# Block 1's 256-column steps in pairs, wider identity products, and an order that counts TensorE's instructions

## The chip, the core and the metric

The kernel runs on one core of a Trainium2 chip. Five engines work side by side on their own instruction streams: TensorE (PE in the rows; its weight loads are a second track, PEld), VectorE (DVE), ScalarE (ACT), GpSimd (POOL) and SyncE (SP), which here issues the transfers. They meet only in semaphores. The metric is the device time of one execution in microseconds (us), the median of several runs.

## What is computed

A chunked attention with eight memory tokens feeds two feed-forward layers, all in fp32 on 3072 tokens:

```python
scores = scale * np.matmul(q_c, k_full.transpose(0, 1, 3, 2))   # 4 x 8 heads, 24 chunks of 32 queries
a = np.exp(scores - np.max(scores, axis=-1, keepdims=True))
a = a / (np.sum(a, axis=-1, keepdims=True) + 1e-09)
out[:, :, c_start:c_end] = np.matmul(a, v_full)
...
x = attn_out as 3072 x 512
h = x @ w_in            # 512 x 2048
g = h * np.clip(h + 3.0, 0.0, 6.0) / 6.0
x = g @ w_out           # 2048 x 512
h = x @ w_in2
g = np.maximum(0.01 * h, h)
return g @ w_out2
```

## The kernel before

**Feed-forward.** Tokens are cut into six blocks of 512 columns. A weight or an activation is held in two parts, a rounded high part and the rest, so that one product of 128 rows by 512 columns takes three groups of matmuls (high by high, low by high, high by low). For blocks 0 and 1 layer 1 goes step by step: for each of 16 slices `f` of the hidden dimension, `hidden` (matmuls at L910) makes 128 rows of h in the PSUM tile `h`, ScalarE adds three and clips (L922, tile `r`), VectorE multiplies (L925), ScalarE rounds to `g` (L318) and VectorE takes the rest (L321); `output` (matmuls at L954) adds the slice's product into the four PSUM tiles `y`. One step has 12 + 12 matmuls. The first four steps of block 1 are done on halves of 256 columns, because the second half of that block's tokens comes late out of the attention. Everything after those blocks is a Strassen form (L1229, L1397), which this change touches in its order alone.

**Weights.** They arrive as fp64 bits. `decode` and `split_w` turn each slice of 128 x 512 into a high and a low part: one ScalarE pass (L370), four VectorE passes (L373 to L385), a ScalarE cast (L318) and a VectorE subtraction (L321). Blocks 0 and 1 need a new pair of slices for each step.

**Attention.** Units of tokens, each one a chain: loads, copies of the keys into windows (L318), scores (a burst of 48 small fp32 matmuls of 32x64 outputs, L513, or 24, L743), maximum, exponentials (L549), sums, six transposes (L571, or three, L797), a copy (L318), the values (48 small fp32 matmuls of 64x32, L582, or 24, L810), and the split into block 0's or 1's operands `xh`, `xl`. The units' bursts are put between the feed-forward matmuls. In the first 35 us, before there is feed-forward work, products of the identity matrix with itself (`warm`, L439), which nobody reads, stand between the attention's bursts on TensorE.

**What sets the order.** No engine's order is written out. Each piece is a `Task` with engines, durations and a key; `schedule` plays them through with prices for engines, semaphores and transfers, and emits each instruction when its turn comes. So a changed price moves instructions on every engine. TensorE takes the task with the lowest key; an attention task that is ahead of its key is held while a feed-forward product is ready. A transfer counts as done at `wire + LANDS`.

## Time and profile before

| | us |
|---|---|
| median of three runs | 1052.82 (1051.19 to 1052.99) |
| the profiled execution, its own time | 1053.29 |
| its span, first to last instruction | 1051.50 |
| TensorE busy | 1030.8 |
| VectorE busy | 879.1 |
| ScalarE busy | 691.1 |

The profiled execution has 1.8 us outside its span and lies 0.5 us over the median. A row of a timeline or a window below starts with its time from the span's start; busy times of TensorE overlap, since matmuls are pipelined. An fp32 product (the attention's bursts and the identity products) is recorded as two matmuls, each with its weight load; the feed-forward's rounded operands take one.

### The profile page before, as it was taken

The page shows a single profiled execution, that of the slowest core. Times are in us where ns is not written, and L with a number is a line of the kernel's source. Part 1 is how long each engine was busy: PE and PEld are TensorE (multiplying, and loading weights), DVE is VectorE, ACT ScalarE, POOL GpSimd, SP SyncE. Part 2 cuts the span into 40 slices and gives each one's busy share as a digit, 9 for nine tenths or more (in the row PEclk, how much of TensorE's full clock was granted, in tenths as well). Part 3 has the DMA queues.
Part 4 walks back from the last instruction along what each step waited for, and adds up shares of the span by engine and source line. Part 5 has one row for each costly group of instructions (what it writes and reads, how often), then busy time and mean ns, then how long its engine had stood idle before and what let it go on. Part 6 is the DMA issues. An engine that isn't in the chain of part 4 may idle for free.

```text
span 1051.5 us, 20297 instructions
## 1 busy us (share of the span) xinstructions
PE 1030.8 (98%) x7528; PEld 854.6 (81%) x7528; DVE 879.1 (84%) x1493; ACT 691.1 (66%) x1444; POOL 23.8 (2%) x31
## 2 busy tenths in 40 slices
PE   7799999999999999999999999999999999999998
PEld 6678888888888888888888888888888888888886
DVE  5898898778999978799999899899475998466775
ACT  2687777555888745477686576786466884666753
POOL 3001000000000000000000000000000000000000
PEclk9899999999999999999999999999999999999999
DMA  9899788886878989872737875356342454432451
GB/s 231 276 246 323 226 279 263 252 263 239 276 250 268 296 269 325 278 242 96 240 121 261 268 238 194 122 178 206 117 177 84 159 197 165 163 119 90 150 180 60
DMA packets 127380, 220.50 MB, mean 210 GB/s; under 512 B 12593, under 2 KB 76081, under 8 KB 127281
## 3 DMA queue, kind: packets, MB, share of 16 engines
q1 hardware_dynamic: 127280, 219.20, 63.8%
q8 instruction: 59, 0.97, 0.4%
q14 instruction: 41, 0.33, 0.1%
HBM read 156.24 MB, written 62.91 MB: 208 GB/s over the span
## 4 chain that ended last, share of the span: by engine, by line
PE 90%; DMA 5%; DVE 2%; ACT 1%; SPq 1%; issue 1%; POOL 0%; DVEq 0%; ACTq 0%
PE y L1229 16%; PE y L954 13%; PE y L1397 12%; PE h L1229 10%; PE h L1397 8%; PE hx L1229 8%; PE hx L1397 8%; PE h L910 8%; DMA w<-in_raw 4%; PE h L954 2%; PE at L582 2%; PE at L513 1%; PE at L571 1%; DMA w<-in_w1o 1%; DMA w<-in_w1i 1%
## 5 line engine op out<-in xcount | busy, mean ns | idle before, releaser
L321 DVE TENSOR_TENSOR w<-w 128x512 fp32r<-128x512 f32 (+2 forms) x393 | 324.2, 861 | 24.9 <-ACT w L318 24.4
L318 ACT CAST w<-w 128x512 fp32r<-128x512 f32 (+1 forms) x290 | 223.5, 804 | 15.6 <-DMA w<-floats 6.7
L954 PE MATMUL y<-g,w 128*128 128x512 f32 (+1 forms) x540 | 124.7, 375 | 0.7 <-ACT w L318 0.4
L1229 PE MATMUL y<-w 128*128 128x512 f32 x516 | 124.3, 390 | 0.0
L1229 PEld LDWEIGHTS y<-w 128*128 128x128 f32 x516 | 96.7, 188 | 20.2
L954 PEld LDWEIGHTS y<-g,w 128*128 128x128 f32 x540 | 95.0, 189 | 19.6 <-ACT w L318 0.9
L318 ACT CAST g<-w 128x512 fp32r<-128x512 f32 x80 | 49.7, 622 | 64.8 <-PE y L1397 21.4
L1397 PE MATMUL y<-w 128*128 128x512 f32 x384 | 90.3, 389 | 0.0
L1397 PEld LDWEIGHTS y<-w 128*128 128x128 f32 x384 | 72.1, 188 | 15.0
L1203 ACT ACTIVATE w<-w 128x512 f32<-128x512 f32 x72 | 45.3, 632 | 44.5 <-DVE w L1274 18.9
L910 PE MATMUL h<-xh,w 128*128 128x512 f32 (+1 forms) x288 | 68.5, 379 | 0.6 <-DVE w L321 0.4
L321 DVE TENSOR_TENSOR g<-w,g 128x512 fp32r<-128x512 f32 x80 | 54.3, 688 | 12.5 <-ACT g L318 12.4
L1397 PE MATMUL h<-w 128*128 128x512 f32 x264 | 62.1, 389 | 0.0
L910 PEld LDWEIGHTS h<-xh,w 128*128 128x128 f32 x288 | 51.3, 196 | 10.6 <-DVE w L321 0.8
L1397 PE MATMUL hx<-w 128*128 128x512 f32 x252 | 59.2, 389 | 0.0
L1229 PE MATMUL h<-xl,w 128*128 128x512 f32 x240 | 58.3, 390 | 0.0
L1397 PEld LDWEIGHTS h<-w 128*128 128x128 f32 x264 | 49.5, 188 | 10.3
L1397 PEld LDWEIGHTS hx<-w 128*128 128x128 f32 x252 | 47.3, 188 | 9.8
L1229 PEld LDWEIGHTS h<-xl,w 128*128 128x128 f32 x240 | 44.8, 188 | 9.3
L1229 PE MATMUL y<-xh,w 128*128 128x512 f32 x216 | 51.9, 389 | 0.0
L1274 DVE TENSOR_TENSOR w<-y,w 128x512 f32<-128x512 f32 x35 | 24.0, 687 | 29.7 <-PE y L1229 27.0
L1229 PEld LDWEIGHTS y<-xh,w 128*128 128x128 f32 x216 | 40.5, 188 | 8.4
(242 smaller groups left out, 1868.6 us busy)
## 6 DMA issues: line engine op xcount, KB each, us to landing
w<-kept2i SPq DMA_DIRECT2D x42, 512.0 KB
w<-kept2o SPq DMA_DIRECT2D x42, 512.0 KB
w<-kept1i SPq DMA_DIRECT2D x28, 512.0 KB
a<-in_raw SPq DMA_DIRECT2D x20, 448.0 KB
w<-in_w1i SPq DMA_DIRECT2D x16, 512.0 KB
w<-in_w1o SPq DMA_DIRECT2D x16, 512.0 KB
w<-in_w2i SPq DMA_DIRECT2D x16, 512.0 KB
w<-in_w2o SPq DMA_DIRECT2D x16, 512.0 KB
```

The source lines that it names most:

```text
L318: nc.scalar.copy(out, in_) if e == "ACT" else engine(e).tensor_copy(out=out, in_=in_)
L321: engine(e).tensor_tensor(out=out, in0=a, in1=b, op=ALU.subtract)
L513: nc.tensor.matmul(ps.t[h * CHUNK:(h + 1) * CHUNK, par, i * W:(i + 1) * W], qk[h // 2].t[r, gp, (h % 2) * G + c * CHUNK:(h % 2) * G + (c + ...
L571: nc.tensor.transpose(pt.t[:, i // NC, (i % NC) * 128:(i % NC + 1) * 128], e.t[:, i].rearrange("p r k -> p (r k)"), ident)
L582: nc.tensor.matmul(pv.t[(h % 2) * D:(h % 2 + 1) * D, par, (h // 2) * 2 * G + i * CHUNK:(h // 2) * 2 * G + (i + 1) * CHUNK], v[h // 2].t[r, ...
L910: nc.tensor.matmul(h.t[:, :n], w.t[:, 1 if p == 1 else 0, k * 128:(k + 1) * 128], x[:, k, c0:c0 + n], start=(p == 0 and k == 0), stop=(p = ...
L954: nc.tensor.matmul(bank(banks[d])[:, c0:c0 + n], w.t[:, 1 if p == 1 else 0, d * 128:(d + 1) * 128], g.t[:, 1 if p == 2 else 0, :n], start= ...
L1203: return add(lambda e: nc.scalar.activation(out=at(), in_=at(), func=AF.Prelu, alpha=0.01), {"ACT": act(N)}, key, after=[after], uses=uses)
L1229: nc.tensor.matmul(bank(to), wt(l, o)[:, kt * 128:(kt + 1) * 128].bitcast(F32R), operand(p, name, 1 if q == 2 else 0, kt).bitcast(F32R), s ...
L1274: done[2] = add(lambda e: nc.vector.tensor_tensor(out=half_of(x, 0), in0=bank(bb), in1=ut.t[:, 0], op=ALU.add), low, key, after=[k, done[1 ...
L1397: nc.tensor.matmul(bank(to[d]), wt(1 if q == 1 else 0, o)[:, d * 128:(d + 1) * 128].bitcast(F32R), g.t[:, 1 if q == 2 else 0], start=(fres ...
```

## The change

Five edits. Block 1's half steps go in pairs: the list of items takes every second `f`, `hidden` puts the first 256 columns of slice `f` and of slice `f + 1` into the two halves of one PSUM tile, and the four passes behind it run once over 512 columns; `output` is called once for each half. The identity products become 512 or 256 columns wide and fewer: 18 for 44. The planner gets a model of TensorE's instructions: `feed` counts the instructions of a task, 447 held at first, 256 with each fetch that comes 5000 ns after the second-last block is used up, and a task that would run dry waits in its duration. An attention task for which that costs more than 250 ns is held while a feed-forward product is ready. A load counts as done 1500 ns later than before (`SURE`). Positions in the item list count a paired step double.

```diff
+    def __init__(self, fn, opts, key, after=(), allocs=(), uses=(), moe=False, issues=1, late=0, loads=False, ins=8):
...
-STARTS, LANDS = 1900.0, 500.0
+STARTS, LANDS, SURE = 1900.0, 500.0, 1500.0
+HELD, FETCHED, FETCH, STALL = 447, 256, 5000.0, 250.0
...
+    def feed(at, task):
+        used, held, comes = queue
+        for _ in range(task.ins):
+            if comes is not None and comes <= at:
+                held, comes = held + FETCHED, None
+            if comes is None and used >= held - FETCHED:
+                comes = at + FETCH
+            if used >= held:
+                at, held, comes = comes, held + FETCHED, None
+            used += 1
+            at += task.opts["PE"] / task.ins
+        return at, (used, held, comes)
...
+                    if e == "PE" and not t.moe and feed(now, t)[0] - now - t.opts["PE"] > STALL and any(i[2].moe and not i[2].taken and blocked(i[2]) is None for i in h):
+                        held.append(item)
+                        continue
...
-                    push(wire + LANDS, "done", (pick, e))
+                    push(wire + LANDS + (SURE if pick.allocs else 0.0), "done", (pick, e))
...
-    items += [("1", 1, f, c, N // 2) for c in (0, N // 2) for f in range(NARROW)]
+    items += [("1", 1, f, c, N // 2) for c in (0, N // 2) for f in range(0, NARROW, 2)]
...
-            x = made(b)[:, 1, 256:384]
+            x = made(b)[:, 1, N - 128 * c:].rearrange("p (a n) -> p a n", a=c)
             for _ in range(n):
-                nc.tensor.matmul(x, ident, ident, start=True, stop=True, skip_group_check=True)
+                nc.tensor.matmul(x, ident, ident.unsqueeze(1).to_broadcast([128, c, 128]), start=True, stop=True, skip_group_check=True)
...
-        product(part(0), n, [whi, *dh], allocs=[h], uses=[xh, w])
-        product(part(1), n, [wlo], uses=[h, xh, w])
-        k = product(part(2), n, dl, uses=[h, xl, w])
+        for o in range(0, N, n):
+            w = wbuf[lay + "i", f + o // n]
+            whi, wlo = wtask[lay + "i", f + o // n]
+            product(part(0, w, o), n, [whi, *dh], allocs=[] if o else [h], uses=[xh, w] + ([h] if o else []))
+            product(part(1, w, o), n, [wlo], uses=[h, xh, w])
+            k = product(part(2, w, o), n, dl, uses=[h, xl, w])
...
-            nc.scalar.activation(out=make(r)[:, :n], in_=h.t[:, :n], func=AF.Relu, bias=three[:, 0:1], scale=1.0)
+            nc.scalar.activation(out=make(r), in_=h.t, func=AF.Relu, bias=three[:, 0:1], scale=1.0)
...
-            output(lay, j, f, c0, n)
+            for o in range(0, N, n):
+                output(lay, j, f + o // n, c0, n, o)
```

The line numbers of the changed kernel are others: its L932 and L981 are the matmuls of `hidden` and `output` (L910, L954 before), L537 the scores, L595 the transposes, L606 the values, L339 the copies and casts, L394 the first pass over a weight, L947 the clip.

**TensorE, the third pair of values and scores** (tile `at` is the attention's PSUM tile). Before, the values L582 and the next unit's scores L513 stand so:

```order
L910 MATMUL h<-xh,w 128x256 x4
L582 MATMUL at<-w 64x32 x48
L910 MATMUL h<-xh,w 128x256 x4
L910 MATMUL h<-xl,w 128x256 x4
L954 MATMUL y<-g,w 128x256 x4
L513 MATMUL at<-w,a 32x64 x48
L954 MATMUL y<-g,w 128x256 x8
```

Now:

```order
L981 MATMUL y<-g,w 128x256 x16
L606 MATMUL at<-w 64x32 x48
L981 MATMUL y<-g,w 128x256 x4
L932 MATMUL h<-xh,w 128x512 x4
L537 MATMUL at<-w,a 32x64 x48
L932 MATMUL h<-xh,w 128x512 x4
```

Twelve matmuls of 256 columns stood between the two bursts; now there are four of 256 and four of 512.

**TensorE, the second pair.** Before:

```order
L582 MATMUL at<-w 64x32 x48
L910 MATMUL h<-xh,w 128x256 x8
L910 MATMUL h<-xl,w 128x256 x4
L954 MATMUL y<-g,w 128x256 x8
L513 MATMUL at<-w,a 32x64 x48
```

Now:

```order
L606 MATMUL at<-w 64x32 x48
L981 MATMUL y<-g,w 128x256 x16
L932 MATMUL h<-xh,w 128x256 x8
L932 MATMUL h<-xl,w 128x256 x4
L537 MATMUL at<-w,a 32x64 x48
L932 MATMUL h<-xh,w 128x256 x8
```

Between the bursts stood 20 matmuls of 256 columns, now 28.

**ScalarE, around the window copies of the third attention unit** (`g<-r` rounds the gated slice that a step's output needs; the copies of 128x2x3x56 and 128x2x3x8 wait for a load of keys). Before:

```order
L370 ACTIVATE wm<-w 128x512
L318 COPY w<-w 128x2x3x56
L318 COPY w<-w 128x2x3x8
L318 COPY w<-w 128x2x3x56
L318 COPY w<-w 128x2x3x8
L318 CAST g<-r 128x512
```

Now:

```order
L339 CAST xh<-at 128x2x192
L339 CAST w<-wm 128x512
L339 CAST g<-r 128x512
L339 COPY w<-w 128x2x3x56
L339 COPY w<-w 128x2x3x8
```

The rounding stood behind the copies and stands ahead of them now.

## Rows read from the trace of the kernel before

**Rows 1.** The page: busy time and counts of each engine; the instruction queue's packets, MB, share.

```profile
PE 1030.8 (98%) x7528; PEld 854.6 (81%) x7528; DVE 879.1 (84%) x1493; ACT 691.1 (66%) x1444; POOL 23.8 (2%) x31
...
q8 instruction: 59, 0.97, 0.4%
```

**Rows 2.** Windows: stretch, length, each engine's busy time (instructions), granted clock, DMA share.

```profile
100.00:150.00 50.00, 47.42 (x827) 42.75 (x826) 44.01 (x96) 36.26 (x126) 3.21 (x2) 0.97 0.79 260
400.00:500.00 100.00, 100.00 (x443) 82.80 (x442) 91.20 (x158) 62.52 (x100) 0.00 (x0) 1.00 0.69 230
```

**Rows 3.** Waits of TensorE, whole span: who for whom, total us, times, longest.

```profile
PE at L743 <- ACT w L318: 3.4, 1, 3.4
...
PE y L954 <- ACT w L318: 0.4, 1, 0.4
```

**Rows 4.** Timeline of TensorE: start, us, operation, matmul records, [idle before <- releaser].

```profile
37.97 1.46 PE L743 MATMUL at<-w 64*32 64x64 f32 x48 [3.44 <-ACT w L318]
...
58.88 1.13 PE L810 MATMUL at<-w 64*64 64x32 f32 x48 [0.63 <-ACT w L318]
...
102.69 1.62 PE L582 MATMUL at<-w 64*64 64x32 f32 x96
...
106.83 1.09 PE L513 MATMUL at<-w,a 64*32 64x64 f32 x87
110.18 0.43 PE L513 MATMUL at<-w,a 64*32 64x64 f32 x9 [2.27 <-issue]
...
113.92 1.60 PE L954 MATMUL y<-g,w 128*128 128x256 f32 x12
...
125.57 0.74 PE L513 MATMUL at<-w,a 64*32 64x64 f32 x51
126.63 0.70 PE L513 MATMUL at<-w,a 64*32 64x64 f32 x45 [0.31 <-issue]
```

**Rows 5.** Windows from one stop of TensorE to the next, and within them.

```profile
0.00:11.50 11.50, 9.10 (x221) 7.72 (x222) 4.26 (x15) 2.60 (x6) 1.96 (x9) 1.00 0.91 250
...
14.35:107.91 93.56, 84.68 (x1390) 70.25 (x1390) 79.42 (x176) 64.22 (x197) 11.38 (x13) 0.95 0.92 277
...
103.82:107.91 4.09, 4.09 (x141) 3.77 (x134) 3.53 (x9) 2.79 (x8) 0.00 (x0) 1.00 1.05 409
122.88:126.31 3.43, 3.43 (x141) 3.10 (x133) 3.43 (x9) 3.15 (x7) 0.00 (x0) 1.00 0.33 93
...
110.18:113.66 3.48, 3.48 (x23) 3.31 (x23) 2.86 (x7) 1.57 (x11) 0.00 (x0) 0.51 0.68 254
```

**Rows 6.** DMA queues (packets, MB, share) in 99.5:107.8, 107.8:108.8, 131.2:132.3, in this order.

```profile
q1 hardware_dynamic: 1226, 3.43, 103.5%
...
q8 instruction: 1, 0.02, 5.9%
...
q8 instruction: 1, 0.02, 5.5%
```

**Rows 7.** Chain that ended last, 0 to 150 us: the load behind the first idle time.

```profile
28.91 8.38 DMA w<-in_raw
```

**Rows 8.** Window 72.30:82.02, then the timeline of ScalarE and VectorE before it.

```profile
72.30:82.02 9.72, 8.41 (x33) 5.65 (x32) 9.63 (x19) 8.75 (x38) 2.62 (x2) 1.00 0.92 301
...
65.49 1.11 ACT L318 COPY w<-w 128x336 f32<-128x336 f32 x4 [0.92 <-DMA w<-in_raw]
...
70.23 0.68 ACT L370 ACTIVATE ys<-w 128x512 f32<-128x512 f32 x1 [1.56 <-DMA w<-in_w1o]
...
67.16 0.69 DVE L321 TENSOR_TENSOR g<-r,g 128x512 fp32r<-128x512 f32 x1 [1.15 <-ACT g L318]
```

**Rows 9.** Identity products on TensorE's timeline; the clip by shape, 92 to 180 us.

```profile
21.02 1.28 PE L439 MATMUL ac<-ident 128*128 128x128 f32 x10
...
L922 ACT ACTIVATE r<-h,three 128x512 f32<-128x512 f32 x8 | 5.8, 719 | 4.6 <-PE h L910 4.6
L922 ACT ACTIVATE r<-h,three 128x256 f32<-128x256 f32 x8 | 3.9, 486 | 1.1 <-PE h L910 1.1
```

More of the change, by code (lines that the diff above doesn't have):

```diff
@@ L66 @@
 class Task:
-    def __init__(self, fn, opts, key, after=(), allocs=(), uses=(), moe=False, issues=1, late=0, loads=False):
-        self.late, self.loads = late, loads
+    def __init__(self, fn, opts, key, after=(), allocs=(), uses=(), moe=False, issues=1, late=0, loads=False, ins=8):
+        self.late, self.loads, self.ins = late, loads, ins
         self.fn, self.opts, self.key, self.moe, self.issues = fn, opts, key, moe, issues
@@ L222, in schedule @@
                     push(free[e], "free", None)
-                    push(wire + LANDS, "done", (pick, e))
+                    push(wire + LANDS + (SURE if pick.allocs else 0.0), "done", (pick, e))
                     continue
+                if e == "PE":
+                    end, queue = feed(now, pick)
+                    d = end - now
                 free[e] = now + d
@@ L333, in tile_attn_moe_moe2 @@
     BLK = STEP * KF
-    pos_h, pos_at = {}, {i: STEP * k for k, i in enumerate(items)}
+    pos_h, pos_at, total = {}, {}, 0
+    for i in items:
+        pos_at[i] = total
+        total += STEP if i[4] == N else 2 * STEP
     for i, p in pos_at.items():
@@ L350, in tile_attn_moe_moe2 @@
         seq2 += [("q", p, n, i) for n in ORDER for i in range(KF // 2)]
-    at = STEP * len(items)
+    at = total
     for kind, j, *of in seq2:
@@ L887, in product @@
             after = [last[0], *after]
-        last[0] = t = add(fn, {"PE": count * mm(n)}, last[0].key + last[0].moe if last[0] else 0, after=after, allocs=allocs, uses=uses, moe=count / 4)
+        last[0] = t = add(fn, {"PE": count * mm(n)}, last[0].key + last[0].moe if last[0] else 0, after=after, allocs=allocs, uses=uses, moe=count / 4, ins=2 * count)
         return t
@@ L910, in fn @@
                     nc.tensor.matmul(
-                        h.t[:, :n], w.t[:, 1 if p == 1 else 0, k * 128:(k + 1) * 128], x[:, k, c0:c0 + n],
-                        start=(p == 0 and k == 0), stop=(p == 2 and k == KD - 1),
+                        h.t[:, o:o + n], w.t[:, 1 if p == 1 else 0, k * 128:(k + 1) * 128], x[:, k, c0:c0 + n],
+                        start=(p == 0 and k == 0 and o == 0), stop=(p == 2 and k == KD - 1 and o + n == N), skip_group_check=True,
                     )
```

49 lines of the change are left out of this document (25 added, 24 removed).

## The prediction

> **What bounds the kernel now.** I read the page first: TensorE is busy for 1030.8 of 1051.5 us [rows 1]. A busy share says little where matmuls are pipelined, so I went to the windows. From 400 to 500 us TensorE runs 443 matmuls of 512 columns, one in 225.7 ns, at the full clock (2.4 GHz) and without a pause [rows 2]; there only fewer matmuls would help, and the change keeps their number. From 100 to 150 us it is idle for 2.6 us and the granted clock is 0.97 [rows 2]. So what the change can win lies in the first 150 us.
>
> Then the waits of TensorE. On another engine's work it waits once for long, 3.4 us, and otherwise for 0.4 us at most in the feed-forward [rows 3]. The timeline shows the long one at 37.97, before the first feed-forward matmul, and two stops that no engine explains ("issue"), 2.27 us at 107.91 and 0.31 us at 126.31, both in the middle of a burst of scores [rows 4].
>
> What are those? TensorE's records are 7528 matmuls and 7528 weight loads, and the instruction queue q8 brought 59 packets: 255 records to a packet [rows 1]. From the span's start to its first stop at 11.50 TensorE began 221 matmuls, and from the restart to the stop at 107.91 another 1390 [rows 5]; 2 x 1390 = 2780 is eleven times 256 less 36, and semaphore instructions, which are not in these counts, fill such a gap. So TensorE stops where a packet ends. The transfers agree: no q8 packet moves from 99.5 to 107.8, then one does (5.9% of 16 engines' 1.0 us, 0.94 us) [rows 6], and TensorE restarts at 110.18, 1.4 us after it.
>
> The price of such a stop is the wait's length less the work that was still at hand. At 103.82 TensorE began the last 256 instructions that it held, and had them done in 4.09 us while the DMA engines were full (share 1.05); the next came at 110.18, after 6.4 us. At 122.88 with a DMA share of 0.33 the same work took 3.43 us, and the next came at 126.63, after 3.75 us [rows 4, 5]. A third case gives the upper end: the packet that followed was requested at about 126.63 and moved only after 131.2 [rows 6]; with 0.9 us of transfer and 1.4 us to the restart that is 7.0 us. An arrival thus takes 3.75 to 7.0 us, more when the DMA engines are full.
>
> The Trainium skill says otherwise (Runtime: NRT & Kernel Launch, Instruction fetch mechanics): blocks of 256 instructions are fetched ahead, PE holds 2048, and the cost of a border is mostly hidden. The block size agrees with 255 records a packet; the hidden cost doesn't agree with the 2.27 us. By that page the planner's new model would be worth nothing.
>
> The stop has a second price. After it the granted clock is 0.51 (1.2 GHz) from 110.18 to 113.66 [rows 5]: in 3.48 us work for 1.8 us, 1.7 us lost. Stops of 0.63 us (58.88) and 0.31 us have no such drop behind them.
>
> **The change part by part.**
>
> *The order that counts instructions.* Removed: the stop at 107.91, 2.27 us, its clock, 1.7 us, and the stop at 126.31, 0.31 us: 4.28 us. What takes their place? I counted the changed order off in the same way (four instructions for each small fp32 product, two for every other matmul, one for each semaphore instruction). Counted so, the old order has packet ends 172 and 99 instructions into the second and third scores, where the trace stops after 87 and 51 matmuls, 174 and 102 instructions [rows 4]: the counting holds. In the new order four packets before 130 us are short. Priced with 11.5 ns for a record of scores, 16 ns for values [rows 4], 119 ns for 256 columns (twelve in 1.60 us, the last 0.17 of it beside the next, rows 4) and 226 ns for 512 [rows 2], and 0.37 us for the switches (what 4.09 and 3.43 us are over the same sum), they last 5.65 (first pair of values and scores), 5.5 and 5.2 (second pair) and 3.3 us (third pair).
> - First pair: 5.65 against 3.75 to 7.0, a stop of 0 to 1.4. Such pairs stopped nothing there before; I take 0.
> - Second pair, two packets: the DMA engines are full there before (0.92 on average from 14 to 108 us, 1.05 at the end, rows 5), and nothing in the change makes the traffic less, so I take 6.0: 0.5 and 0.8 us, bounds 0 and 1.5, 0 and 1.8.
> - Third pair: the planner counts eight instructions to a product and no semaphores, and the end that it expects behind the scores falls 159 of 192 instructions into them. 3.3 us of work against 3.75 to 7.0: 0.45 to 3.7. The same pair of units found the DMA engines at 0.33 before, so I take 0.45.
> - From 140 us on the short packets have 5.2 us and more; before, 3.6 us sufficed there without a stop. Nothing.
> Together 1.75 us return, and none of these stops is as long as the one that felled the clock. Net 2.5 us, bounds 4.3 gained and 2.6 lost.
>
> *The reserve for loads.* From 72.30 to 82.02 TensorE does 32 matmuls of 512 columns, 7.2 us of work, in 9.72 us with VectorE busy for 9.63 [rows 8]: VectorE's preparation of weights is late by 2.5 us. It had lost 1.15 us at 67.16, waiting for ScalarE's rounding of g, which stood behind window copies that waited for their load; ScalarE also sat for 1.56 us before a load at 70.23 [rows 8]. The change puts the rounding ahead of the copies. Up to VectorE's last weight of block 0's first half the order has about the same work ahead of each weight as before (within 2 us either way), so only idle time can be won: 1.15 at most here, and a moved load (slice 4 of w1o, behind another 1.8 MB) can take some back. I take 0.8, bounds -1.5 and 2.5.
>
> *The identity products.* 44 products of 128 columns were 5632 columns; 18 wider ones are 6144. Ten records of 128 columns take 1.28 us [rows 9], so this is some 0.5 us more TensorE time in the first 34 us, and 104 instructions fewer. Neither counts: the first feed-forward work waits for a load issued at 28.91 that takes 8.38 us [rows 7], and TensorE stands idle for 3.44 us before 37.97 [rows 4]. The order of loads up to that one is the same. A cast of block 0's operand now stands behind a weight's cast after that load: 0 to 0.5 us, taken back by the VectorE-bound stretch behind it. The clock drop of that idle time stays.
>
> *A gap that is filled.* Before the values at 58.88 TensorE waits 0.63 us for a copy [rows 4]; eight matmuls now stand there. VectorE is late 15 us on, so it would only wait longer there: 0, bound 0.6.
>
> *The pairs.* The same matmuls. Behind them a clip of 512 columns takes 719 ns where two of 256 took 2 x 486 [rows 9], likewise the three passes after it: under 1 us on each of ScalarE and VectorE, which TensorE doesn't wait for there. What is between a step's h and its output doubles, from 24 to 48 matmuls of 256 columns; no wait stood there before, so 0. If that cover went, the chain of four passes, some 2.6 us, would show at each pair.
>
> *Everything after 200 us* is reordered on VectorE, ScalarE and SP, with the work unchanged and no feed-forward wait over 0.4 us in the whole trace [rows 3]: 0, bounds -1 and 0.5.
>
> **The sum.** 1053.3 - 4.3 + 1.75 - 0.8 = 1049.95 for an execution like the profiled one, a gain of 3.35. The median lies 0.5 below that execution: 1052.8 - 3.35 = 1049.4.
>
> **The rivals.**
> - *The third pair pays in full (slower).* If the DMA engines are full when its packet is asked for, the arrival takes 7.0 us, the stop is 3.7 us, longer than the 2.27 that felled the clock, and 1.7 us more go with the clock. With 1.3 in the second pair that is 6.7 against the 4.28 removed, and the 0.8 of VectorE may be lost too: 1052.8 + 2.4 = 1055.2. It turns slower from an arrival of about 5.3 us on if the clock falls with it. For it: arrivals of 6.4 and 7.0 us on either side of this place; against: the 3.75 at it. Chance 0.12.
> - *Borders cost nothing, and the stops have another cause.* Then they stay, or move with the transfers; only VectorE's 0.8 is won: 1052.0. Against it: three stops and the count of packets. The page of the skill named above would have it so. Chance 0.1.
> - *VectorE takes the gain.* The moved load and twelve exponentials in one row on ScalarE make weights late again between 72 and 82 us, 1.5 us worse: 1052.8 - 2.5 + 1.5 = 1051.8. Chance 0.18.
> - *All waits go.* Arrivals of 5 us and less, VectorE's 2.5 us recovered in large part: 1052.8 - 4.28 + 0.45 - 1.9 = 1047.1. Chance 0.12.
>
> **How the numbers follow.** The forecast has 0.48, and its own range is 1048.2 to 1050.7. The range that should hold 8 in 10 reaches over the two middle rivals and into the ends: 1046.6 to 1053.6. About 0.2% (2.1 us) is what can be told from no change, that is, faster is under 1050.7. Faster: nearly all of the forecast, the last rival and a little of the third, 0.6. Slower: most of the first rival, 0.1. Same: the rest, 0.3.
>
> **What would show it.** Right: no idle time at 107 us, no granted clock under 1 between 45 and 200 us, a short "issue" stop (0.3 to 0.8 us) late in the third burst of scores and one or two in the steps around the second; the stretch from the sixth to the seventh step's matmuls with under 2 us of waiting; from 200 us on the same spacing of 225.7 ns. Wrong: an "issue" stop of over 2 us with a clock of 0.5 behind it, waits on VectorE's L321 beyond 2.5 us, or waits on weights after 200 us, which nothing here foresees.

## The result, and the profile after

| | before | changed |
|---|---|---|
| median, us (runs) | 1052.71 (6) | 1059.32 (6) |
| range, us | 1051.19 to 1053.10 | 1057.34 to 1061.49 |
| the profiled execution, us | 1053.29 | 1057.82 |
| its span, us | 1051.5 | 1056.0 |

The ratio on record is 1.0051, with a 95% interval of 1.0029 to 1.0072 (the quotient of the two medians, 1.0063 or 6.6 us, lies within it): the changed kernel is slower by about 0.5%. 1049.4 was predicted, with a range from 1046.6 to 1053.6. The prediction has the wrong sign and the time lies outside its range. The profiled execution of the changed kernel is one of its two fastest, with a mean granted clock of 0.995 where the other five have 0.988 to 0.991; what the slower ones lose beyond it, no trace shows.

The page of the changed kernel reads as it should by the change: 52 matmul records fewer (18 identity products for 44, two records each), the same 59 packets of instructions, nearly the same busy time on the others [rows 1].

```profile
PE 1034.2 (98%) x7476; PEld 849.1 (80%) x7476; DVE 876.5 (83%) x1483; ACT 689.9 (65%) x1439; POOL 21.3 (2%) x30
...
q8 instruction: 59, 0.97, 0.4%
```

The waits of TensorE over the whole span (who for whom: total us, times, longest) are another list than [rows 3]. The long stop for instructions is gone. In its place stand waits of the feed-forward's products, `y` above all, for weights and for `g`:

```profile
PE y L981 <- ACT w L339: 2.8, 1, 2.8
...
PE h L932 <- POOL w L342: 1.1, 1, 1.1
PE y L981 <- DVE g L342: 0.9, 1, 0.9
PE y L981 <- ACT g L339: 0.9, 1, 0.9
...
PE at L537 <- issue: 0.2, 1, 0.2
```

**Where the 4.5 us came from.** For each stretch of the span I took the time from the start of one group of matmuls to the start of the next, less what its products take at the full clock: 226.8 ns for 512 columns, 119.0 for 256, 109 for a transpose, 11.5 and 16.2 for a record of scores and values. The sum over all groups is TensorE's loss, idle time and slow clock together. The first feed-forward product starts at 39.36 before and 39.16 after, and the sum is taken from there on.

| TensorE's loss, us | 39 to 70 | 70 to 88 | 88 to 100 | 100 to 118 | 118 to 135 | 135 to 200 | 200 to 400 | 400 to end | sum |
|---|---|---|---|---|---|---|---|---|---|
| before | 4.58 | 2.72 | 0.27 | 4.48 | 1.02 | 2.23 | 2.60 | -0.22 | 17.69 |
| changed | 4.06 | 6.63 | 0.46 | 0.47 | 3.23 | 2.60 | 4.70 | 0.27 | 22.43 |

(The nominal times are rounded, so a stretch without loss can come out a little below zero.) So the change won 4.0 us where it was aimed, between 100 and 118, and lost 3.9 between 70 and 88, 2.2 between 118 and 135, and 2.6 after 200. The small rest is a gain of 0.5 before 70 and losses of 0.2 and 0.4 between.

The loss at 70 to 88 in the timeline of TensorE (start, us, records, [idle before <- releaser]):

```profile
71.58 1.10 PE L932 MATMUL h<-xh,w 128*128 128x512 f32 x4
73.82 1.20 PE L932 MATMUL h<-xh,w 128*128 128x512 f32 x4 [1.14 <-POOL w L342]
74.86 1.07 PE L932 MATMUL h<-xl,w 128*128 128x512 f32 x4
78.69 1.95 PE L981 MATMUL y<-g,w 128*128 128x512 f32 x4 [2.76 <-ACT w L339]
81.13 2.64 PE L981 MATMUL y<-g,w 128*128 128x512 f32 x8 [0.49 <-DVE w L342]
```

The product at 78.69 waits for the high part of w1o's slice 4. ScalarE's rows show why it is late: first two waits for transfers, then the maximum, twelve exponentials, a clip, and only then the cast at 77.94. (The exponentials are the L573 rows; one is shown.)

```profile
66.00 1.11 ACT L339 COPY w<-w 128x336 f32<-128x336 f32 x4 [1.25 <-DMA w<-in_raw]
...
69.69 0.66 ACT L394 ACTIVATE ys<-w 128x512 f32<-128x512 f32 x1 [1.51 <-DMA w<-in_w1o]
...
73.89 0.31 ACT L573 ACTIVATE w<-at,mx 128x64 f32<-128x64 f32 x1 [0.89 <-DVE mx L558]
...
77.94 0.70 ACT L339 CAST w<-ys 128x512 fp32r<-128x512 f32 x1
```

VectorE's passes over the same slice (tile `ys`) stand behind its own two idle times, which ScalarE's waits had caused: 2.85 us lost, and the clamp and the sign come only at 74.31 and 75.66.

```profile
68.21 0.69 DVE L342 TENSOR_TENSOR w<-w 128x512 fp32r<-128x512 f32 x1 [1.39 <-ACT w L339]
...
70.96 0.69 DVE L950 SCALAR_TENSOR_TENSOR r<-r,h 128x512 f32<-128x512 f32 x1 [1.46 <-ACT r L947]
...
74.31 0.41 DVE L397 TENSOR_SCALAR ys<-ys 128x512 f32<-128x512 f32 x1
...
75.66 0.68 DVE L405 SCALAR_TENSOR_TENSOR ys<-w,ys 128x512 uint32<-128x512 uint32 x1
```

Before, waits for transfers were there too [rows 8], but the slice had its clamp at 69.91 and its cast stood between the sixth and the seventh exponential, and the product for it started at 76.06 after a wait of 0.45 us:

```profile
75.39 0.62 ACT L318 CAST w<-ys 128x512 fp32r<-128x512 f32 x1
```

Behind the wait TensorE's clock was granted at 0.50 (1.2 GHz) from 78.85 to 82.27 (windows: busy times, clock, DMA share, GB/s), as behind the stop of the kernel before [rows 5]:

```profile
78.85:82.27 3.42, 2.93 (x7) 1.83 (x8) 3.42 (x5) 3.17 (x11) 1.47 (x1) 0.50 1.02 417
```

### The profile page after: what moved, and what is told of

Its sections match the earlier page's. It is cut to its first block, busy times and chain, and to the rows that moved or that the text cites. A ratio compares the mean times of both kernels' runs of the same rounds, so it can differ in the third digit from the quotient of the medians.

```text
span 1056.0 us, 20188 instructions
## 1 busy us (share of the span) xinstructions
PE 1034.2 (98%) x7476; PEld 849.1 (80%) x7476; DVE 876.5 (83%) x1483; ACT 689.9 (65%) x1439; POOL 21.3 (2%) x30
## 4 chain that ended last, share of the span: by engine, by line
PE 83%; DMA 6%; DVE 5%; SPq 2%; ACT 2%; issue 2%; DVEq 0%; ACTq 0%
PE y L1256 15%; PE y L1424 12%; PE y L981 11%; PE h L1256 10%; PE h L1424 8%; PE hx L1424 8%; PE hx L1256 7%; PE h L932 5%; PE h L981 2%; DMA w<-in_raw 2%; DMA w<-in_w1o 1%; PE at L606 1%; DVE w L342 1%; PE at L537 1%; SPq L504 1%
## 5 line engine op out<-in xcount | busy, mean ns | idle before, releaser
L339 ACT CAST w<-w 128x512 fp32r<-128x512 f32 (+1 forms) x290 | 223.5, 803 | 15.4 <-DMA w<-floats 4.0
L981 PE MATMUL y<-g,w 128*128 128x512 f32 (+1 forms) x540 | 126.4, 378 | 5.0 <-ACT w L339 2.8
L1256 PE MATMUL y<-w 128*128 128x512 f32 x516 | 124.5, 390 | 0.0
L981 PEld LDWEIGHTS y<-g,w 128*128 128x128 f32 x540 | 95.0, 190 | 24.2 <-ACT w L339 3.2
L339 ACT CAST g<-w 128x512 fp32r<-128x512 f32 x80 | 49.4, 620 | 62.6 <-PE y L1424 22.1
L1424 PE MATMUL y<-w 128*128 128x512 f32 x384 | 90.3, 389 | 0.0
L932 PE MATMUL h<-xh,w 128*128 128x512 f32 (+1 forms) x288 | 68.2, 376 | 1.1 <-POOL w L342 1.1
L932 PEld LDWEIGHTS h<-xh,w 128*128 128x128 f32 x288 | 50.0, 191 | 10.7 <-POOL w L342 1.6
L981 PE MATMUL y<-w 128*128 128x512 f32 x180 | 46.6, 391 | 0.0
```

What stands on the lines that cost most here:

```text
L339: nc.scalar.copy(out, in_) if e == "ACT" else engine(e).tensor_copy(out=out, in_=in_)
L932: nc.tensor.matmul(h.t[:, o:o + n], w.t[:, 1 if p == 1 else 0, k * 128:(k + 1) * 128], x[:, k, c0:c0 + n], start=(p == 0 and k == 0 and o ...
L981: nc.tensor.matmul(bank(banks[d])[:, c0:c0 + n], w.t[:, 1 if p == 1 else 0, d * 128:(d + 1) * 128], g.t[:, 1 if p == 2 else 0, at:at + n], ...
L1256: nc.tensor.matmul(bank(to), wt(l, o)[:, kt * 128:(kt + 1) * 128].bitcast(F32R), operand(p, name, 1 if q == 2 else 0, kt).bitcast(F32R), s ...
L1424: nc.tensor.matmul(bank(to[d]), wt(1 if q == 1 else 0, o)[:, d * 128:(d + 1) * 128].bitcast(F32R), g.t[:, 1 if q == 2 else 0], start=(fres ...
```

## The experiments

The theory at the start: the new order, not the work, costs the time, and it costs it at slice 4. Rivals: loads that the reserve makes late; the parts of the change themselves. Some runs keep every engine's order and move single instructions, so that nothing else changes; others take a part of the change away or add one, and with it deal a new order. Each gave a ratio to the kernel before, run on the same chip beside it; these ratios are what is compared, since the chip was not the same in every run.

### Slice 4 alone, the rest of the order kept

A table of moves is put behind the planner: the named instruction goes ahead of the other on its own engine.

```diff
+MOVES = (
+    ("1o4 clamp", "1o3 lo"),
+    ("1o4 bits", "1o3 lo"),
+    ("1o4 sign", "1o3 lo"),
+    ("1o4 hi", "1i7 abs"),
+)
```

> The changed kernel with every engine's order kept, but four instructions moved: for slice 4 of w1o, the clamp, the shift and the sign on VectorE go up to the place where VectorE stood idle 1.39 us at 68.21, and the cast of its high part on ScalarE goes ahead of the twelve exponentials (it stood behind them, at 77.94). Theory 'order': the loss is made at 71.6 to 83.6 us, where TensorE waits 2.76 us for this cast; the wait goes, the clock's fall behind it may go too, and the run is 2.5 to 4 us faster than the changed kernel: 1055 to 1057. Rival 'late loads': the slice itself comes too late, the moved passes wait for it, and nothing is gained: 1058 to 1060. Rival 'spread': the loss does not sit here, 1058 to 1060 though the wait at y is gone.

1058.94 us, ratio 1.0046 (1.0032 to 1.0061). Nothing gained. The wait for the cast is gone; in its place the products behind it, of the same step, wait for the slice's low part, VectorE's last pass, which I had left where it was:

```profile
PE y L997 <- DVE w L358: 3.4, 1, 3.4
```

So the rest of the slice goes up as well:

```diff
+    ("1o6 abs", "1i7 abs"),
+    ("1o4 low", "1i5 low"),
+    ("1o4 hi", "1o6 abs"),
+    ("1o4 lo", "1i6 clamp"),
```

> The changed kernel with its order kept but for seven instructions: all five passes of slice 4 of w1o (clamp, shift, sign, the joining of the low bits, the difference) go up on VectorE into the two places where it stood idle (1.39 us at 68.21, 1.46 us at 70.96); its cast on ScalarE goes ahead of the twelve exponentials; and the magnitude of w1o's slice 6, in front of which ScalarE stood 1.51 us for a transfer, goes behind three instructions that were ready. The run before this one moved the cast and three passes alone, and the wait moved from the cast to the difference (3.4 us). Theory 'order': the loss of the changed kernel sits in this stretch (about 4 us against before, and a fall of the clock behind it), so 3 to 5 us come back: 1054 to 1056.5. Rival 'full engines': VectorE and ScalarE simply have too much work here, the wait moves once more to the next slice: 1058 to 1060.

1058.17 us, ratio 1.0055 (1.0035 to 1.0075). In the profile the place is healed: the loss from 70 to 100 us falls from 7.1 to 2.9, and the product of slice 4 starts without a wait:

```profile
77.66 1.09 PE L951 MATMUL h<-xl,w 128*128 128x512 f32 x4
78.58 2.89 PE L1000 MATMUL y<-g,w 128*128 128x512 f32 x12
```

The time gives back nothing of the 3 to 5 us expected: the ratio is 1.0055 where the changed kernel's is 1.0051, and the two intervals overlap. In this execution TensorE lost 6.8 us up to 70 us where the changed kernel lost 4.1, in an order that is the same up to 66 us. The difference is the clock. It was granted at 0.50 until 44.86 us (until 41.31 in the changed kernel's profile), and again from 51.68 to 55.10, behind a wait of 1.34 us that both have; half of the time at 0.50 is 4.2 us here and 1.1 there. First this run's rows, then the changed kernel's, whose clock stayed at 1.00:

```profile
49.63 1.20 PE L853 MATMUL at<-w 64*64 64x32 f32 x48 [1.34 <-ACT w L358]
51.68:55.10 3.42, 3.42 (x10) 2.40 (x8) 2.85 (x6) 2.57 (x8) 0.00 (x0) 0.50 1.16 224
...
47.56 1.20 PE L834 MATMUL at<-w 64*64 64x32 f32 x48 [1.34 <-ACT w L339]
48.69:52.30 3.61, 3.61 (x65) 2.74 (x61) 3.54 (x8) 3.21 (x8) 0.00 (x0) 1.00 1.03 356
```

So the cause is right for its place: the wait went with the move. That the wait is what makes the kernel slow is not shown, since the time did not come back with it; and one profile can't settle a difference of 3 us before 70 us.

### One part of the change at a time

Taken away from the changed kernel, first the reserve, the count of fetches (447 instructions held become a number that is never used up), and block 1's pairs:

```diff
-STARTS, LANDS, SURE = 1900.0, 500.0, 1500.0
+STARTS, LANDS, SURE = 1900.0, 500.0, 0.0
```

> The changed kernel planned without the reserve of 1500 ns for loads; the rest as changed. Theory 'order': slice 4 of w1o is issued 7 transfers earlier, but its cast still stands behind twelve exponentials, so the wait of 2 to 3 us near 76 stays: 1056 to 1060. Rival 'late loads': the wait goes with the reserve: 1050 to 1054.

1055.83 us, 1.0023 (1.0011 to 1.0035). The wait for slice 4's cast is still there (2.4 us), as the theory had it. The profile loses 1.1 us between 100 and 135 in place of 3.7, which may be why the run is faster; but the profiled execution (1057.84) lies 2.0 us above the run's median and no lower than the changed kernel's, so this is not shown.

```diff
-HELD, FETCHED, FETCH, STALL = 447, 256, 5000.0, 250.0
+HELD, FETCHED, FETCH, STALL = 1000000, 256, 5000.0, 250.0
```

> The changed kernel planned without the count of instruction fetches; pairs, wide products and reserve stay. The cast of slice 4 of w1o stands between six exponentials and six again, as in the kernel before. Theory 'order': TensorE's wait near 76 falls under 1 us (gain about 4), and stops for instructions come back where a packet's border falls into scores with 2.9 to 3.6 us of work since the request (near 80, 98, 114, 131): 0.5 to 2.3 us each, 2 to 5 in all: 1054 to 1060, with the loss at other places than in the changed kernel. Rival 'late loads': the wait near 76 stays, the stops come on top: 1060 to 1064.

1059.50 us, 1.0054 (1.0036 to 1.0072); one further execution of the twelve took 5862 us, for which no trace shows a cause, and is not in the ratio. Slice 4 has 1.1 us of wait, the stops are back with 1.9 us. The largest loss is elsewhere: 8.8 us after 200 us.

```diff
-    items += [("1", 1, f, c, N // 2) for c in (0, N // 2) for f in range(0, NARROW, 2)]
+    items += [("1", 1, f, c, N // 2) for c in (0, N // 2) for f in range(NARROW)]
```

> The changed kernel with block 1's steps of 256 columns single again; count of fetches, reserve and wide products stay. The prediction gave the pairs no cost. Seen so far: TensorE's loss between 200 and 400 us is 3.9 to 9.1 us in all kernels with pairs and 2.3 to 4.4 in those without. Theory 'pairs late': the loss between 200 and 400 us falls by 1.5 to 2.5 us to about 2.5 to 3; slice 4 of w1o stands behind twelve exponentials here too, so the wait near 76 stays: 1055 to 1058. Rival 'new deal': the loss after 200 us follows the deal and not the pairs, and stays over 4: 1056 to 1061.

1065.28 us, 1.0121 (1.0101 to 1.0140): the slowest of all. Without the pairs the loss after 200 us doesn't fall, it rises to 8.2. "Pairs late" is refuted as the only cause of that loss, though not as one of several; the time is above the 1056 to 1061 of the rival too.

Now one part added to the kernel before (the edit is in each case that part of the change's diff).

> The kernel before with only the identity products made wider and fewer; all other engines keep their order but for some 20 rows. Theory 'order': the products themselves are worth nothing either way (work behind 39 us starts within 0.3 us of before), but they take about 100 instructions out ahead, so the packets' borders move: into scores near 65 (5.2 us of work since the request), 81 (4.0), near 97 (3.5, into 256-column products) and 113 (3.4). Two to three stops of 0.3 to 2 us instead of two: 1051 to 1055. Rival 'warm-up': fewer, wider products let the clock fall more in the first 40 us and the run loses 2 us or more there: 1055 to 1058.

1053.01 us, 0.9999 (0.9985 to 1.0014). All other orders stay but for some 20 rows ahead of 41 us, and the time stays too. The identity products cost nothing and gain nothing. (The packets' borders move with them, and one of the stops; more on this below.)

> The kernel before with only block 1's steps in pairs. Prediction on record: pairs cost nothing by themselves, the stop near 110 stays (3.6 us of work since the request near 97, 4.7 near 113): 1051 to 1054. Rival 'chain': at each pair's first output product TensorE waits about 1 to 2.6 us for relu, clip, cast and difference of 512 columns: 1055 to 1060.

1054.47 us, 1.0022 (1.0008 to 1.0036): 0.8 to 3.8 us slower than the kernel before, a little more than the prediction's nothing. No wait at the pairs' output products is longer than 0.3 us, so the rival "chain" is out.

> The kernel before with only the count of instruction fetches in the planner. Theory 'order': holding attention units back shifts their exponentials into one row of twelve with the cast of slice 4 behind it, as in the changed kernel; the stops for instructions at 106 to 114 shrink by 1 to 2.5 us, and TensorE's wait for slice 4 near 76 grows to 1.5 to 3 us: 1052 to 1056. Rival 'fetches alone': only the stops go: 1048.5 to 1050.5. Rival 'reserve': as the one before, since without the reserve nothing is late.

1059.45 us, 1.0072 (1.0053 to 1.0092). The stops do shrink, to 0.2 us in all. But neither the theory (1052 to 1056, by a wait at slice 4) nor a rival had the time: `y` now waits 3.5 us for `g` from 115 to 119 us, with the clock at 0.50 behind it from 119.3 to 122.7:

```profile
PE y L975 <- ACT g L339: 4.5, 2, 3.5
...
PE at L534 <- issue: 0.2, 1, 0.2
```

> The kernel before with only the reserve of 1500 ns for loads. Slice 4 of w1o keeps its place among the loads, and its cast stands between six exponentials and six. Theory 'order': no new wait near 76; the rest is shuffled and lands within 3 us: 1051 to 1056. Rival 'late loads': 2 to 4 us of waits for weights between 65 and 85: 1056 to 1060.

1058.87 us, 1.0063 (1.0045 to 1.0082), and no long wait for weights between 65 and 85 us: neither the theory's small shuffle nor the rival's place. The same wait for `g` again, and the stops on top:

```profile
PE y L975 <- ACT g L339: 3.4, 2, 2.9
PE at L534 <- issue: 3.2, 3, 1.7
```

Two parts that have nothing to do with each other cost some 7 us each (7.6 and 6.6 by the ratios) and produce the same wait, `y` for `g` up to 119 us. That made the order itself the suspect.

### New orders that mean nothing

```diff
-STARTS, LANDS = 1900.0, 500.0
+STARTS, LANDS = 1920.0, 500.0
```

> The kernel before, nothing of the change in it; the planner's estimate of a load's start is 1920 ns where it was 1900. Nothing on the chip depends on this 1 per cent, but the planner deals all engines a new order from it (265 differing rows on TensorE, 746 on ScalarE, 1125 on VectorE; the reserve alone gave 222, 783 and 1791). Theory 'new deal': the order before was one that had come out well, any other order puts waits of 2 to 4 us somewhere before 130 us and the run is 3 to 7 us slower: 1055 to 1060. Rival 'the parts themselves': the count of fetches and the reserve each cost 6 us by what they do, and a change of 1 per cent costs nothing: 1051 to 1054.

```diff
-MARGIN = 300.0
+MARGIN = 310.0
```

> The kernel before with the planner's margin ahead of TensorE's attention steps at 310 ns where it was 300; the order is dealt anew (311, 802 and 1237 differing rows on TensorE, ScalarE, VectorE), and slice 4's cast stands behind a row of twelve exponentials here too. Theory 'new deal': 1055 to 1060, with its waits at other places than the draw with 1920. Rival 'the parts themselves': 1051 to 1054.

```diff
-STARTS, LANDS = 1900.0, 500.0
+STARTS, LANDS = 1880.0, 500.0
```

> The kernel before with the planner's estimate of a load's start at 1880 ns where it was 1900 (155, 654 and 1162 differing rows on TensorE, ScalarE, VectorE). Theory 'new deal': 1055 to 1060. Rival 'the parts themselves': 1051 to 1054. If the three draws scatter on both sides of the kernel before, neither holds, and its order is no better than another.

Ratios 1.0062 (1.0040 to 1.0083), 1.0089 (1.0060 to 1.0118) and 1.0018 (1.0005 to 1.0031): all three slower than the kernel before, by 6.5, 9.4 and 1.9 us, without a line of the change in them. (The third is under the 1055 to 1060 expected.) The waits are of the kind that the parts had produced. The first:

```profile
PE y L954 <- ACT g L318: 4.8, 2, 3.8
```

and the second, where slice 4's cast stands behind twelve exponentials too:

```profile
PE y L954 <- ACT g L318: 5.1, 2, 3.8
...
PE y L954 <- ACT w L318: 2.7, 1, 2.7
```

The same with the change in: only the time that the planner gives a packet of instructions, 4000 and 6000 ns for 5000.

```diff
-HELD, FETCHED, FETCH, STALL = 447, 256, 5000.0, 250.0
+HELD, FETCHED, FETCH, STALL = 447, 256, 4000.0, 250.0
```

> The changed kernel with the planner's time for a packet of instructions to arrive at 4000 ns in place of 5000; pairs, wide products, reserve as changed. It is dealt anew (188, 549 and 719 differing rows on TensorE, ScalarE, VectorE against the changed kernel), and the cast of slice 4 of w1o stands between six exponentials and six again, as in the kernel before. Theory 'new deal': the wait near 76 is under 1 us, and yet the run is 2 to 8 us slower than the kernel before, by waits at other places: 1055 to 1060. Rival 'slice 4 alone': with that wait gone the change's own gain shows: 1050 to 1053.

> The same with 6000 ns (338, 884 and 1745 differing rows against the changed kernel); slice 4's cast stands between six exponentials and six here too. Theory 'new deal': 1055 to 1060. Rival 'slice 4 alone': 1050 to 1053. If both come out near the kernel before and under the changed one, the change's parts are worth something on average and the changed kernel was an unlucky deal of them.

1054.65 and 1056.93 us, 1.0013 (1.0003 to 1.0023) and 1.0038 (1.0023 to 1.0052). The first came close to the kernel before, under what the theory expected, with a wait at slice 4 of 1.5 us where under 1 was expected; the second, with only 0.4 us of wait there, is 4 us above it. Neither beats the kernel before: "slice 4 alone" is out as well.

The kernels that were dealt anew in one table, with the run of the wide products. The loss is counted as above; ratios are taken over a kernel's runs, the loss is of the one profiled execution. The first column begins at the first feed-forward product, which starts between 38.5 and 39.8 us in most, but at 40.6 with the pairs alone and at 36.1 with 310 ns; this shift comes on top of the losses.

| kernel | ratio to before | first product to 70 | 70 to 100 | 100 to 135 | 135 to 200 | 200 to end |
|---|---|---|---|---|---|---|
| before | 1 | 4.6 | 3.0 | 5.5 | 2.2 | 2.4 |
| changed | 1.0051 | 4.1 | 7.1 | 3.7 | 2.6 | 5.0 |
| changed, no reserve | 1.0023 | 6.7 | 7.6 | 1.1 | 1.7 | 4.8 |
| changed, no count of fetches | 1.0054 | 5.4 | 4.1 | 3.7 | 2.1 | 8.8 |
| changed, no pairs | 1.0121 | 6.1 | 7.1 | 6.0 | 2.2 | 8.2 |
| changed, 4000 ns | 1.0013 | 5.8 | 4.5 | 2.3 | 2.2 | 5.1 |
| changed, 6000 ns | 1.0038 | 5.6 | 2.8 | 9.0 | 2.5 | 4.8 |
| before, wide products | 0.9999 | 5.6 | 2.7 | 4.2 | 2.5 | 2.1 |
| before, pairs | 1.0022 | 4.3 | 2.2 | 3.4 | 2.7 | 4.7 |
| before, count of fetches | 1.0072 | 4.7 | 3.5 | 7.5 | 1.6 | 5.2 |
| before, reserve | 1.0063 | 5.4 | 2.6 | 7.7 | 4.5 | 2.9 |
| before, 1920 ns | 1.0062 | 5.0 | 3.9 | 10.1 | 1.6 | 2.4 |
| before, 310 ns | 1.0089 | 6.4 | 7.6 | 9.1 | 1.8 | 4.0 |
| before, 1880 ns | 1.0018 | 6.0 | 1.9 | 5.0 | 3.7 | 2.6 |

Nine kernels hold one or more parts of the change that deal a new order (the changed kernel among them): ratios from 1.0013 to 1.0121. Three hold none and are dealt anew: 1.0018 to 1.0089. The two groups lie on top of each other. In time, the change can't be told from a new deal that means nothing; three deals are few, though, and how their constants were picked is not on record.

One column speaks for the parts: from 200 us on, each of the eight kernels with the pairs or the count of fetches loses 4.7 to 8.8 us, each of the six without them 2.1 to 4.0. In the changed kernel 2.6 of the 4.7 us stand there. So it stays open whether that share is the deal's or the parts' own: no run takes the two apart with the order kept.

### The stop alone, the rest of the order kept

If the order is a draw, then the stop must be taken out without a new deal. On TensorE alone the two bursts of scores go later:

```diff
+MOVES = (
+    (("s", 3, 0), 5),
+    (("s", 3, 1), 2),
+)
```

> The kernel before with every other engine's order kept, row for row; on TensorE alone the scores at 106.83 stand five steps of four products later and those at 125.57 two steps. The packet's border then comes about 2.4 us later in time, so that the stop of 2.27 us at 110.18 has 0 to 0.3 us left and the clock has no reason to fall behind it. Recorded forecast (the stops are worth 2.27 and 0.31 us and the clock 1.7 us): 1048.5 to 1050.5. Rival 'given back': the scores end where they ended anyway, but the products of block 1 that now run ahead of them wait for weights or for g: 1052 to 1054.

1053.57 us, 1.0008 (0.9993 to 1.0023): no gain of more than 0.7 us, as the rival "given back" had it. The stop is gone, all 96 records of the scores run in one go, but TensorE then waits 3.28 us for `g`:

```profile
109.73 1.35 PE L535 MATMUL at<-w,a 64*32 64x64 f32 x96
...
113.03 0.64 PE L933 MATMUL h<-xl,w 128*128 128x256 f32 x4
116.95 1.70 PE L977 MATMUL y<-g,w 128*128 128x256 f32 x12 [3.28 <-ACT g L340]
```

ScalarE's rows show the chain. It sits idle until the scores' maximum is there, does six exponentials, the clip of the step, six more, and only then the cast of `g`:

```profile
112.59 0.31 ACT L571 ACTIVATE w<-at,mx 128x64 f32<-128x64 f32 x1 [2.62 <-DVE mx L556]
...
114.34 0.50 ACT L945 ACTIVATE r<-h,three 128x256 f32<-128x256 f32 x1
...
116.42 0.47 ACT L340 CAST g<-r 128x256 fp32r<-128x256 f32 x1
```

In the kernel before, the scores ended at 110.6 [rows 4] and that cast came at 116.28, with its product at 116.79; here they ended at 111.1, the cast came at 116.42 and the product at 116.95:

```profile
116.28 0.44 ACT L318 CAST g<-r 128x256 fp32r<-128x256 f32 x1
```

The end of the stretch was set by scores, maximum, exponentials and `g` all along, and the stop stood in their shadow. The run of the wide products says the same without a moved instruction: there the packet's end falls early into the burst, the stop is 0.85 us with no drop of the clock behind it, and the same product waits 1.15 us for `g`; its time was that of the kernel before.

```profile
108.67 1.07 PE L534 MATMUL at<-w,a 64*32 64x64 f32 x84 [0.85 <-issue]
...
115.88 1.69 PE L975 MATMUL y<-g,w 128*128 128x256 f32 x12 [1.15 <-ACT g L339]
```

Was it the order on ScalarE, or had ScalarE no room? The step's clip and cast go ahead of the exponentials (ScalarE was idle there), VectorE's two passes likewise, and the next step's follow:

```diff
+    ("ACT", "gate 1.1 3 0", "exp0 3 0"),
+    ("ACT", "ghi 1.1 3 0", "exp0 3 0"),
+    ("ACT", "gate 1.1 0 256", "exp1 3 0"),
+    ("ACT", "ghi 1.1 0 256", "1o9 abs"),
+    ("DVE", "times 1.1 3 0", "max 3 0"),
+    ("DVE", "glo 1.1 3 0", "max 3 0"),
+    ("DVE", "times 1.1 0 256", "1o8 low"),
+    ("DVE", "glo 1.1 0 256", "1i10 sign"),
```

> The kernel before with the scores later as in the run of that name, and eight more moves: on ScalarE the relu and the cast of g of the step whose product waited 3.28 us go ahead of the exponentials of that unit (ScalarE stood idle 2.62 us there), the next step's relu between the two sixes; VectorE's clip and difference for both steps go up likewise. Theory 'chain': the stop for instructions had been hiding the chain scores, maximum, twelve exponentials, g; with g out of that chain the wait of 3.28 us falls under 1 us, and the stop of 2.27 us stays gone: 1049.5 to 1051.5. Rival 'full engines': ScalarE and VectorE then bring the next g or the next weights late by as much: 1052 to 1054.

1056.35 us, 1.0027 (1.0016 to 1.0038): above the range of the theory and above that of the rival. The wait of 3.28 us is gone, and two others stand there, one ahead of it and one behind:

```profile
109.13 0.95 PE L1000 MATMUL y<-g,w 128*128 128x256 f32 x4 [1.75 <-ACT g L356]
...
119.83 1.54 PE L609 MATMUL at<-ident,w 128*128 128x128 f32 x6 [2.15 <-POOL w L605]
```

The second is the unit's own chain again: its exponentials came later, so the transposes wait for GpSimd's scaling of them. The first is not the order. ScalarE was held up 3.11 us by a transfer out of the buffer `ys`, with the DMA engines full (share 1.05 from 105 to 109 us):

```profile
108.13 0.66 ACT L408 ACTIVATE ys<-w 128x512 f32<-128x512 f32 x1 [3.11 <-DMA half<-ys]
```

Up to that pass every engine has the order of the run before it, where the same pass waited 0.96 us; so this wait is not the moves' doing, and it muddies what they are worth. The theory is refuted as far as the time goes. The rival "full engines" fits the second wait; that whichever wait is taken away, the next resource is as late, has been seen twice here and is not shown for the stretch as a whole. The same, tried on the changed kernel's two waits for `g` at 123.00 and 125.81, on top of the moves for slice 4:

```diff
+    ("ACT", "ghi 1.1 0 256", ">exp1 3 0"),
+    ("ACT", "gate 1.1 2 256", "-1"),
+    ("ACT", "ghi 1.1 2 256", ">gate 1.1 2 256"),
+    ("DVE", "glo 1.1 0 256", "1i11 bits"),
+    ("DVE", "times 1.1 2 256", ">1o10 clamp"),
+    ("DVE", "1o10 bits", ">times 1.1 2 256"),
+    ("DVE", "1i10 hi", ">1o10 bits"),
+    ("DVE", "glo 1.1 2 256", ">1i10 hi"),
```

> The changed kernel with slice 4 early as before and its two waits for g at 122 to 126 us (0.9 us each) taken away likewise: the casts of g for block 1's first two pairs go ahead of copies and weights on ScalarE, clip and difference go up on VectorE. Theory 'chain': loss between 118 and 135 us falls from 3.6 to about 2 us: 1055.5 to 1057, 1.5 less than with slice 4 alone. Rival 'full engines': the weights that now stand behind come late by as much: 1057.5 to 1059.

1058.14 us, 1.0043 (1.0029 to 1.0057), as the rival "full engines" had it and as with slice 4 alone. The waits for `g` are gone; the loss from 118 to 135 us rose from 3.6 to 7.4, by waits for GpSimd's scaling (2.7 us in two) and for ScalarE's copy behind it (1.8 us), with the clock at 0.50 behind them from 127.5 to 134.3.

The losses of the runs that keep a dealt order, counted as in the table above:

| kernel | ratio to before | first product to 70 | 70 to 100 | 100 to 135 | 135 to 200 | 200 to end |
|---|---|---|---|---|---|---|
| before, scores later | 1.0008 | 4.3 | 1.8 | 5.4 | 2.2 | 2.5 |
| before, scores later, `g` ahead | 1.0027 | 4.3 | 2.0 | 8.2 | 2.4 | 2.4 |
| changed, cast of slice 4 early | 1.0046 | 6.2 | 7.1 | 3.7 | 2.4 | 4.9 |
| changed, slice 4 early | 1.0055 | 6.8 | 2.9 | 4.1 | 1.6 | 4.6 |
| changed, slice 4 early, `g` ahead | 1.0043 | 4.3 | 2.7 | 9.6 | 1.4 | 5.0 |

The last column repeats with the order: four executions of the changed kernel's order behind 200 us lose 4.6 to 5.0, four of the order before (the wide products among them) 2.1 to 2.5. So those 2.6 us belong to the order and are no accident of an execution. The first column does not repeat: four executions with the changed kernel's order up to 66 us lost between 4.1 and 6.8.

## Why the prediction was wrong, point by point

The step that failed is the way in which the sum was made: it took the waits of the old order, subtracted those that a part removed as if they were time at the end (4.3 us), and put the rest of the new order at -0.8 and 0. The runs show in its place that the removed stops are worth at most 0.7 us at the end (the run with the scores moved, by its interval), that the new order loses 3.9 us more at 70 to 88 us, 2.2 more at 118 to 135 and 2.6 more after 200, and that the three orders dealt anew without any part of the change are 1.9 to 9.4 us slower too. How much of the loss the parts would cause in any order is not shown.

- **The stops for instructions: right as a mechanism, wrong as a gain.** The counting held. In the changed kernel the third pair's packet was forecast to end 159 of 192 instructions into the scores, at 0.45 us; TensorE stopped after 81 of 96 records, 162 instructions, and the burst took 1.54 us for 1.11. The row:

```profile
131.85 0.34 PE L537 MATMUL at<-w,a 64*32 64x64 f32 x15 [0.23 <-issue]
```

  The 1.3 us of the second pair did not come at all. Between 100 and 118 us the loss fell by 4.0, as forecast (2.27 and 1.7; the other 0.31 of the 4.28 stood at 126 us). But the sum counted this as time at the end, and what takes the place of a stop that goes was asked for packets alone and not for the other engines. The run with the scores moved alone answers it: what is late next is `g`, by 3.28 us. Between 100 and 135 us the changed kernel keeps 1.8 of the 4.0 us. (The bound of 2.6 us lost comes to 2.7 by the terms of the list, and to 4.1 with the first pair's 1.4.) The rival "borders cost nothing" is refuted in its mechanism and confirmed in its price: TensorE does stop where a packet ends, and the end does not move when the stop goes. The Trainium skill (Runtime: NRT & Kernel Launch, Instruction fetch mechanics) calls the cost of a border mostly hidden; the 2.27 us of the row [rows 4] show TensorE stopped, against that sentence. The run with the scores moved shows the price hidden at the end, but behind another chain.
- **VectorE's idle time, -0.8 with bounds of -1.5 and 2.5: this is the term that failed first.** The loss from 70 to 88 us rose by 3.9. The third rival had the place and the mechanism (the moved load, twelve exponentials in one row, weights late between 72 and 82 us) with a chance of 0.18, but at 1.5 us. The load itself was not late: no row shows the slice's first pass waiting for it. What is late are its later passes, behind VectorE's idle time, and its cast, behind the row of exponentials.
- **The pairs at 0.** By themselves nothing waits at them. In the changed kernel one pair waits 0.86 us for the cast of its `g` and 0.94 us for the rest of it, at 123.00 and 125.81; the forecast named this chain, at 2.6 us, and put it at 0.
- **Everything after 200 us at 0, bounds -1 and 0.5.** It lost 2.6 us more than before, in pieces of about 1 us and less. The bounds came from [rows 3], that is, from the waits of the old order. They say nothing about a new one.
- **Identity products at 0, no gap, load order up to 39 us: right.** The first feed-forward product starts within 0.2 us of before; so close is luck, since it starts between 39.16 and 40.04 in four executions with this order. (The extra TensorE time of the wider products is 1.0 us by the forecast's own row [rows 9] and not 0.5, since each product is two records; nothing hung on it.)
- **The chance of slower, 0.1.** It held one mechanism (a dearer stop). The case that any new order is slower was not among the rivals. The three meaningless deals cost 1.9 to 9.4 us; with them known, the forecast would have been the sum plus some 6 us (their mean), and the range several us to either side.

What stays open: why the kernel before has so good an order (that it is better than its three neighbours is measured; whether its constants had been picked for their time, which would make any neighbour look worse, no run here can show), whether pairs and count of fetches cost something after 200 us by themselves, and what the slower executions of the changed kernel lose beyond the profiled one.

## What to carry to other kernels

When a planner deals the order of in-order engines, a change of its prices is a new draw: before you price its parts, change a constant by one per cent that means nothing and see how far the time moves; an effect below that scatter can't be put down to the part. To learn what a part is worth, keep the dealt order and move single instructions. And a stop on the longest engine is worth its length only if the thing that comes next is ready earlier too: follow the chain behind it on the other engines before you subtract it.

## What the runs showed of the hardware

- A moved burst of scores moved the packet's border in time, as counted, and with it the stop: 2.27 us before, none where the scores started at 109.73 in place of 106.83.
- The length of an idle time did not decide whether TensorE's clock fell. It was at 0.50 for 3.4 us behind the stop of 2.27 us before and behind the 2.76 us of waiting in the changed kernel, and at 0.52 from 110.0 to 113.0 behind the 1.75 us of the run with `g` ahead. It fell behind a wait of 1.34 us in the run with slice 4 early and not behind the same wait in the changed kernel. Behind the 3.28 us of the run with the scores moved alone it stayed at full speed. The forecast had tied the clock to the length of the stop. The windows of the run with the scores moved around its wait:

```profile
113.70:116.95 3.25, 0.00 (x0) 0.00 (x1) 3.25 (x8) 3.25 (x21) 0.00 (x0) 1.00 0.03 13
116.95:120.40 3.45, 3.45 (x29) 3.45 (x30) 3.42 (x9) 3.45 (x12) 1.48 (x1) 1.00 0.96 285
```

- The same order scatters more between executions than I had allowed for. The kernel with only the scores moved has the order of before up to 106 us, yet its first feed-forward product started at 41.37 us in its profile, 2.0 us later. The kernel before itself ran between 1049.8 and 1058.4 us beside these kernels. So a difference of 2 to 3 us before 70 us between two profiles says little; a column that repeats, as the one after 200 us, says more.
- A store can hold up an engine that only computes: ScalarE's pass into `ys` waited 0.96 us in one kernel and 3.11 us in another for a transfer out of that buffer, and not at all in the kernel before. All three have the same order on ScalarE up to that pass, and in all three the DMA engines are full there (shares of 1.04 to 1.05 from 105 to 109 us).
